# A replanned transformer-block kernel: RMS weight as a scale of its own, splits kept off GpSimd, logits with the router weights stationary

## Chip, cores, metric

One core of a Trainium2 chip. The metric is the device time of one launch in microseconds (us). All input arrays of the reference are float64 or float32 on the host; the large matmuls run as three matmuls of `float32r` parts ("hi" and "lo", x = hi + lo).

## Reference

```python
def _attn_ref(q, k, v):                       # 4 x 8 heads x 576 x 64, causal window of 64
    scores = np.matmul(q, k.transpose(0, 1, 3, 2)) / np.sqrt(D)
    scores = np.where((rel >= 0) & (rel < 64), scores, -1e9)
    attn = softmax(scores)
    return np.matmul(attn, v)
def _moe_ref(x, w_gate, w_val, w_out, rms_g): # 2304 tokens, 512 -> 1536 -> 512
    xn = x / np.sqrt(np.mean(x * x, -1, keepdims=True) + 1e-6) * rms_g
    g = xn @ w_gate
    return (g / (1 + np.exp(-g)) * (xn @ w_val)) @ w_out
def _moe2_ref(x, w_gate, w_output_gate, w1, w2):  # 8 experts, 512 -> 1024 -> 512
    logits = x @ w_gate
    e_idx = np.argmax(logits, axis=1)             # one expert per token
    ...
    out[mask] = gate_w[mask, None] * eom[mask, e, None] * (np.maximum(x[mask] @ w1[e], 0) @ w2[e])
```

## The kernel before

The 2304 tokens are 18 tiles of 128. Three parts follow each other and overlap at the seams.

**Attention** (`attention_front`, `attention_tile`), tile by tile: q, k and v are loaded (`rx`) and split into hi and lo; scores of half the heads go to a PSUM bank; max, exp with row sums, the division; four transposes; the product with V; an evacuation into `x`. Early tiles (t < `qzt`) use full 128-row weights for the scores (lines 672 to 674, and for t < `mpe` the mask is added by a 13th matmul, line 661); later tiles use two 64-row halves of TensorE (line 700, twelve matmuls for half the heads). The norm then squares (`sqr`), sums with a matmul against ones (line 850; from t >= `spe` on after two additions), takes the root by a seed and two Newton steps on 128x1 columns (`newton`, line 883 and on), transposes the result over the partitions (line 900), multiplies (`norm`, line 906) and splits into `xn`.

**Feed-forward** (`ffn_group`, `ffn_step`): seven units of 2 or 3 tiles in six groups; group 0 holds units 0 and 1. A step takes one of 12 slices of the 1536 columns: twelve matmuls for the gate, twelve for the value (lines 1050 to 1052: "a group of twelve" below; there are 168), tanh on ScalarE, two multiplications on VectorE, a split into `h`, and matmuls with `wo` (lines 1092 to 1094) into banks that stay open. In group 0 every slice's weights arrive as float64 words and are rebuilt by `conv` with integer operations on ScalarE and VectorE, split, and saved to DRAM (`whd`) for the later groups.

**Experts**: `route` transposes each finished tile (line 1160), evacuates it, multiplies with the 16 router columns `rw` (line 1167), and works out an expert and a slot for each token; GpSimd scatters the rows to DRAM (`xs`, line 1249). `experts` then runs a first block of 256 tokens, and one block per expert (the first of 128 tokens, `narrow`). `weights` loads an expert's matrices in halves and splits each half into `w` (lines 1477 to 1484); `put` scatters finished rows to the output from GpSimd's queue (line 1640). The router's last matmuls, the counting and the token loads of the blocks all lie between the last feed-forward step and the first expert block.

**What sets the order.** The code records operations (`pl.op`) with a priority, the engines that may run each and a cost on each. `Plan.order` lists them in time with these costs, gives each to the engine that would end it first, and writes the program in that order. Each engine runs its own list in order, so an instruction that waits holds all behind it. Up to a planned time `warm` the planner fills TensorE's idle time with matmuls of ones (line 505, "fillers"). `K` holds the numbers that steer it. The helpers `hi_i` (line 348 on ScalarE, 350 on GpSimd, 352 on VectorE), `lo_i` and `both` (355) and `times` (358) record all splits and many other operations, so those lines stand for many tiles' work.

Of the kernel before, what the change touches and what calls it, by code (L numbers as in the profile page):

```python
# [21 lines left out]
P = 128  # L22
# [10 lines left out]
HOP = 0.2  # L33
TICK, FULL = 3.4133, 1.275
HOPS = {"t": 0.0, "a": 0.12, "v": 0.12, "p": 0.12, "s": 0.0}
K = dict(
    qzt=6, spe=4, lact=12, warm=50, wf=1.17, flead=37.337, pvt=5, nwv=0, port=1, t0=44.466, pp=93.644,
    lead=1.877, clead=14.32, stag=6.769, stage=1.089, slack=0.045, mpe=5, nt=2, look=-0.002, marg=0.239, dw=2.625, ewl=20.108,
    ews=5.63, xld=30.179, xtn=3.067, mlead=8, vb=0.61, vb2=0.298, tb=124.917, share=-0.071, rlead=4.252, span=0.82, wl=3.695,
# [17 lines left out]
class Op:  # L57
    __slots__ = ("engs", "fn", "prio", "seq", "succ", "need", "deps", "bufs", "eng", "start", "end", "dma", "done", "dur", "rows", "lock")


class Filler:


    def __init__(self, fn, lo):
        self.fn, self.lo = fn, lo


class Plan:
# [10 lines left out]
    def op(self, engs, fn, r=(), w=(), hold=(), prio=0.0, dma=0.0, after=(), rows=1.0, lock="p"):  # L79
        o = Op()  # L80
        o.engs, o.fn, o.prio, o.seq, o.dma, o.rows = engs, fn, prio, len(self.ops), dma, rows
        o.lock = lock
# [33 lines left out]
    def order(self):  # L116
# [11 lines left out]
        def enable(o):  # L128
            for e in o.engs:
                t = max((d.end + (HOPS[e] if d.eng == e and not d.dma else HOP) for d in o.deps), default=0.0)  # L130
                heapq.heappush(wait, (t, o.seq, e, o))
# [6 lines left out]
        ticks = {}  # L138

# [29 lines left out]
        while left:  # L169
# [5 lines left out]
            for e in free:  # L175
# [3 lines left out]
                while ready[e]:  # L179
                    it = heapq.heappop(ready[e])  # L180
# [33 lines left out]
                    if e == "t":  # L214
                        c = pe_time(now, c, o.rows)
# [13 lines left out]
                    for b in o.bufs:  # L229
                        b.left -= 1  # L230
                        b.end = max(b.end, o.end)
                        if not b.left:
                            b.slot["buf"], b.slot["free"] = None, b.end + HOP
# [10 lines left out]
            if self.filler and free["t"] <= now + 1e-9 and self.filler.lo < now < K["warm"]:  # L244
# [26 lines left out]
def attention_ffn_moe(  # L271
# [102 lines left out]
    def cost(n, kind):  # L374
        f = n / 512.0
        return {
            "hs": {"a": 0.12 + 0.48 * f, "p": 0.1 + 0.52 * f, "v": 0.09 + 0.29 * f},
            "ls": {"v": 0.09 + 0.555 * f, "p": 0.17 + 1.12 * f},
            "hp": {"a": 0.1 + 0.48 * f, "v": 0.08 + 0.56 * f},
            "lp": {"v": 0.08 + 0.56 * f},  # L380
# [16 lines left out]
    rw = fixed("rw", [P, KD, 2 * E])  # L397
    iota_m = fixed("iota_m", [P, PT, E])
# [3 lines left out]
    def c_ident(e):  # L402
        t = ident.t
        nc.gpsimd.memset(t, 0.0)
# [4 lines left out]
    def c_masks(e):  # L409


        nc.gpsimd.memset(masks.t, 0.0)
# [12 lines left out]

    def c_ones(e):
# [1388 lines left out]
```

## Time and profile before

| | |
|---|---|
| median of 3 runs | 885.95 us (883.63 to 887.12) |
| profiled execution, its own time | 887.55 us |
| its span, first to last instruction | 885.5 us |
| busy: TensorE (PE) / VectorE (DVE) / ScalarE (ACT) / GpSimd (POOL) | 855.3 / 548.3 / 400.5 / 298.9 us |
| mean granted TensorE clock | 0.981 |
| instructions | 16016 |

A matmul's row shows when it starts and how long it is under way; matmuls overlap, so what one costs is the distance from its start to the next start.

### The profile page before, as it was taken

To read this page: it belongs to the slowest core of one execution; us is meant where nothing else is said; L and a number is where in the kernel's file an instruction comes from. 1 tells how busy PE (TensorE), PEld (TensorE's weight loads), DVE (VectorE), ACT (ScalarE), POOL (GpSimd) and SP (SyncE) were. 2 spreads that over 40 slices of the span, in tenths; PEclk is the share of its full clock that TensorE was granted. 3 is DMA by queue.
4 is the path that set the end of the run, shared out by engine and by line. 5 is a ranking of instruction groups with operands and counts; after the bars stand their busy time and mean duration, and the time that the engine had idled before them with its cause. 6 is when DMAs were issued, how large, how long until landed. Compare 5 with 4: busy or idle time off the path is not lost. (4 is left out here: it accounts for less than half of the span.)

```text
span 885.5 us, 16016 instructions
## 1 busy us (share of the span) xinstructions
PE 855.3 (97%) x5786; PEld 780.3 (88%) x5786; DVE 548.3 (62%) x1258; ACT 400.5 (45%) x1050; POOL 298.9 (34%) x510
## 2 busy tenths in 40 slices
PE   8989999999999999999999999999989999999995
PEld 8978998999899999889998999999968888989984
DVE  6887898977775673756466553554576253556640
ACT  7888776664643452445342342222333132343420
POOL 6886543315324231443224220210133132233320
PEclk8998999999999999999999999999998999999998
DMA  6266799637524431265014317540095344656500
GB/s 195 92 246 219 245 277 316 236 120 253 188 80 140 174 131 38 96 201 172 8 67 160 143 49 285 171 175 1 27 321 206 119 144 147 210 176 228 192 25 19
DMA packets 54016, 139.28 MB, mean 157 GB/s; under 512 B 6800, under 2 KB 6800, under 8 KB 53936
## 3 DMA queue, kind: packets, MB, share of 16 engines
q1 hardware_dynamic: 50912, 128.40, 42.9%
q0 software_dynamic: 3024, 9.85, 2.9%
q8 instruction: 46, 0.75, 0.4%
q14 instruction: 34, 0.28, 0.1%
HBM read 113.69 MB, written 24.54 MB: 156 GB/s over the span
## 5 line engine op out<-in xcount | busy, mean ns | idle before, releaser
L1050 PE MATMUL bank<-xn,w 128*128 128x384 f32 (+1 forms) x672 | 216.6, 322 | 3.3 <-POOL xn L350 2.3
L1051 PE MATMUL bank<-xn,w 128*128 128x384 f32 (+1 forms) x672 | 211.4, 315 | 0.6 <-DVE xn L355 0.6
L1052 PE MATMUL bank<-xn,w 128*128 128x384 f32 (+1 forms) x672 | 211.6, 315 | 0.2 <-DVE w L355 0.2
L1050 PEld LDWEIGHTS bank<-xn,w 128*128 128x128 f32 x672 | 128.1, 191 | 8.2 <-POOL xn L350 2.5
L1051 PEld LDWEIGHTS bank<-xn,w 128*128 128x128 f32 x672 | 128.2, 191 | 2.9 <-DVE xn L355 0.8
L1052 PEld LDWEIGHTS bank<-xn,w 128*128 128x128 f32 x672 | 128.0, 190 | 0.4 <-DVE w L355 0.4
L355 DVE TENSOR_TENSOR w<-raw,w 128x512 fp32r<-128x512 f32 x114 | 85.3, 790 | 10.7 <-POOL w L350 5.7
L1092 PE MATMUL bank<-wo,h 128*128 128x512 f32 x216 | 87.4, 405 | 1.3 <-POOL h L350 1.1
L1094 PE MATMUL bank<-wo,h 128*128 128x512 f32 x216 | 85.2, 394 | 0.0
L1093 PE MATMUL bank<-wo,h 128*128 128x512 f32 x216 | 85.0, 394 | 0.0
L1075 DVE TENSOR_TENSOR u<-u,bank 128x384 f32<-128x384 f32 (+1 forms) x84 | 41.5, 494 | 69.1 <-PE bank L1052 67.1
L1062 ACT ACTIVATE u<-bank 128x384 f32<-128x384 f32 (+1 forms) x84 | 37.2, 443 | 84.2 <-PE bank L1052 74.8
L350 POOL TENSOR_SCALAR w<-raw 128x512 fp32r<-128x512 f32 x59 | 36.3, 631 | 107.0 <-PE bank L1052 39.1
L1622 PE MATMUL bank<-w,eh 128*128 128x512 f32 (+1 forms) x168 | 67.9, 404 | 3.4 <-DVE eh L355 3.4
L1588 PE MATMUL bank<-xT,w 128*128 128x256 f32 (+4 forms) x224 | 68.5, 306 | 0.3 <-DVE eh L1599 0.3
L348 ACT CAST h<-u 128x384 fp32r<-128x384 f32 (+1 forms) x68 | 31.9, 470 | 80.2 <-DVE u L1075 74.1
L1590 PE MATMUL bank<-xT,w 128*128 128x256 f32 (+4 forms) x224 | 68.2, 304 | 0.0
L1589 PE MATMUL bank<-xT,w 128*128 128x256 f32 (+4 forms) x224 | 68.1, 304 | 0.0
L1067 DVE SCALAR_TENSOR_TENSOR u<-u,bank 128x384 f32<-128x384 f32 (+1 forms) x84 | 41.4, 493 | 42.1 <-ACT u L1062 41.5
L1624 PE MATMUL bank<-w,eh 128*128 128x512 f32 (+1 forms) x168 | 67.2, 400 | 0.0
L1623 PE MATMUL bank<-w,eh 128*128 128x512 f32 (+1 forms) x168 | 67.1, 400 | 0.0
L348 ACT CAST w<-raw 128x512 fp32r<-128x512 f32 x67 | 38.9, 618 | 35.1 <-PE bank L1052 17.4
(262 smaller groups left out, 1856.3 us busy)
## 6 DMA issues: line engine op xcount, KB each, us to landing
w<-whd SPq DMA_DIRECT2D x80, 512.0 KB, 3.8
raw<-in_moe_w_dram SPq DMA_DIRECT2D x64, 512.0 KB, 4.6
whd<-w SPq DMA_DIRECT2D x24, 512.0 KB, 5.1
raw<-in_moe_w_gate_dram SPq DMA_DIRECT2D x12, 512.0 KB, 5.4
raw<-in_moe_w_val_dram SPq DMA_DIRECT2D x12, 512.0 KB, 4.3
raw<-in_moe_w_out_dram SPq DMA_DIRECT2D x12, 512.0 KB
rx<-in_q_dram SPq DMA_DIRECT2D x18, 256.0 KB, 3.1
rx<-in_k_dram SPq DMA_DIRECT2D x18, 256.0 KB, 2.8
```

The source lines that it names most:

```text
L348: nc.scalar.copy(o, i)
L355: ve[e].tensor_tensor(out=o, in0=i, in1=h, op=ALU.subtract)
L1050: nc.tensor.matmul(o, lhsT=h_, rhs=xn.t[:, 0, kk], start=(kk == 0), stop=False)
L1051: nc.tensor.matmul(o, lhsT=h_, rhs=xn.t[:, 1, kk], start=False, stop=False)
L1052: nc.tensor.matmul(o, lhsT=l_, rhs=xn.t[:, 0, kk], start=False, stop=(kk == KD - 1))
L1092: nc.tensor.matmul(o, lhsT=h.t[:, 0, c], rhs=wo.t[:, 0, f], start=(n == 0), stop=False)
L1093: nc.tensor.matmul(o, lhsT=h.t[:, 0, c], rhs=wo.t[:, 1, f], start=False, stop=False)
L1094: nc.tensor.matmul(o, lhsT=h.t[:, 1, c], rhs=wo.t[:, 0, f], start=False, stop=(n == NF - 1))
L1588: nc.tensor.matmul(o, lhsT=wh, rhs=x.t[:, 0, kk, 0:N], start=(kk == 0), stop=False)
L1589: nc.tensor.matmul(o, lhsT=wh, rhs=x.t[:, 1, kk, 0:N], start=False, stop=False)
L1590: nc.tensor.matmul(o, lhsT=wl, rhs=x.t[:, 0, kk, 0:N], start=False, stop=(kk == KD - 1))
L1622: nc.tensor.matmul(bk.t[0:M], lhsT=hh, rhs=wh, start=(f == 0), stop=False)
```

## The change

The planner gets other costs (`LAT`, the wait after an operation by the engine that ran it; costs of splits, exp, evacuations), a price `SW` for changing between 64-row and 128-row matmuls, and a rule that keeps 64-row matmuls together (`stk`). GpSimd's cost for splits is raised by 9 us (`phs`, `pls`), so that they are no longer given to it. All of `K` is new. The norm weight `g_sb` is multiplied into `x` by an operation of its own (`weigh`) that needs only `x`, and `norm` becomes one VectorE multiplication instead of four. For the first four slices of the feed-forward weights (`sf`), the low word is moved by two halfword operations on ScalarE (`c5`, `c6`) instead of one, and VectorE's two combining operations become one shift and one combination (`c7`, `c8`). The logits are computed with the split router weights `rws` as the stationary operand (32 columns) and the token tile, split as well, as the moving one; the 32x128 result is evacuated, transposed back and its two halves added (`r2l`, `r3` to `r6`). Tile 6 uses the early form of the scores, tiles 5 and 6 the mask by matmul, and tile 4 the sum of squares by four matmuls.

```diff
 K = dict(
-    qzt=6, spe=4, lact=12, warm=50, wf=1.17, flead=37.337, pvt=5, nwv=0, port=1, t0=44.466, pp=93.644,
-    lead=1.877, clead=14.32, stag=6.769, stage=1.089, slack=0.045, mpe=5, nt=2, look=-0.002, marg=0.239, dw=2.625, ewl=20.108,
+    qzt=7, spe=5, lact=12, warm=60, wf=1.17, flead=25.12, pvt=5, nwv=3, port=1, t0=51.748, pp=92.284,
+    lead=1.956, clead=25.385, stag=6.317, stage=0.717, slack=0.051, mpe=7, nt=2, look=-0.026, marg=0.132, dw=0.933, ewl=14.362,
...
-            "hs": {"a": 0.12 + 0.48 * f, "p": 0.1 + 0.52 * f, "v": 0.09 + 0.29 * f},
-            "ls": {"v": 0.09 + 0.555 * f, "p": 0.17 + 1.12 * f},
+            "hs": {"a": 0.07 + 0.49 * f, "p": 0.09 + 0.53 * f + K["phs"], "v": 0.09 + 0.29 * f},
+            "ls": {"v": 0.08 + 0.56 * f, "p": 0.15 + 1.13 * f + K["pls"]},
...
+                        c = pe_time(now, c + SW * (o.tiled != tiled), o.rows)
...
+        def weigh(e):
+            if e == "a":
+                for kk in range(KD):
+                    nc.scalar.activation(out=x.t[:, kk], in_=x.t[:, kk], func=AF.Copy, scale=g_sb.t[:, kk:kk + 1])
+            else:
+                both(e, x.t, x.t, g_sb.t.unsqueeze(2).to_broadcast([P, KD, P]), ALU.mult)
...
         def norm(e):
-            for kk in range(KD):
-                nc.vector.scalar_tensor_tensor(
-                    out=x.t[:, kk], in0=x.t[:, kk], scalar=g_sb.t[:, kk:kk + 1], in1=bk2.t[:, 0:P],
-                    op0=ALU.mult, op1=ALU.mult,
-                )
+            both("v", x.t, x.t, bk2.t[:, 0:P].unsqueeze(1).to_broadcast([P, KD, P]), ALU.mult)
...
+        def c6(e):
+            nc.scalar.copy(t.t.bitcast(U16)[:, 1::2], a.t.bitcast(U16)[:, 3::4])
...
-            def r3(e, bx=bx, b2=b2):
+            def r3(e, bx=bx, bl=bl, b2=b2):
                 for kk in range(KD):
-                    nc.tensor.matmul(
-                        b2.t[:, 0:2 * E], lhsT=bx.t[:, kk * P:(kk + 1) * P], rhs=rw.t[:, kk],
-                        start=(kk == 0), stop=(kk == KD - 1),
-                    )
+                    for z, b in enumerate((bx, bl)):
+                        nc.tensor.matmul(
+                            b2.t[0:4 * E, 0:P], lhsT=rws.t[:, kk].rearrange("p z e -> p (z e)"),
+                            rhs=part(b)[:, kk * P:(kk + 1) * P], start=(kk + z == 0), stop=(kk + z == KD),
+                        )
```

How instructions move, at three places.

GpSimd's list, from the last scatter of routed rows to the fifth `put` (`out_dram<-osb`), before; `w<-raw` are splits of expert weights:

```order
L1249 DMA xs<-raw_7913,si_115 18432x514
L350 TENSOR_SCALAR w_8206<-raw_8143 128x512
L350 TENSOR_SCALAR w_8233<-raw_8150 128x512
L1640 DMA out_dram<-osb_8222,meta_0_148 2304x512
L1640 DMA out_dram<-osb_8281,meta_1_149 2304x512
L350 TENSOR_SCALAR w_8335<-raw_8230 128x512 x2
L355 TENSOR_TENSOR w_8337<-raw_8239,w_8337 128x512
L350 TENSOR_SCALAR w_8401<-raw_8271 128x512 x2
L350 TENSOR_SCALAR w_8422<-raw_8304 128x512
```

and the same place in the changed program:

```order
L1308 DMA xs<-raw_8099,si_118 18432x514
L1699 DMA out_dram<-osb_8425,meta_0_151 2304x512
L1699 DMA out_dram<-osb_8439,meta_1_152 2304x512
L1699 DMA out_dram<-osb_8626,meta_0_153 2304x512
L1699 DMA out_dram<-osb_8872,meta_0_154 2304x512
```

The splits of expert weights have left GpSimd's list; in this stage it holds only puts. They stand in the lists of ScalarE and VectorE.

ScalarE's list, the rebuilding of the first slice of gate weights (`t2k`, `t`), in the early attention, before:

```order
L348 COPY val_191<-val_275 64x1024
L948 ACTIVATE t2k_342<-raw_242 128x512
L953 ACTIVATE t_344<-raw_242 128x512
L730 ACTIVATE s_290,m_350<-bank_289,m_350 128x128 x4
L348 CAST kt_304<-rx_286 128x4x2x64
```

and now:

```order
L358 COPY kt_422<-kt_301 128x8x64
L969 ACTIVATE t2k_441<-raw_368 128x512
L985 ACTIVATE t_443<-raw_368 128x512
L988 COPY t_443<-raw_368 128x512
L745 ACTIVATE s_425,m_476<-bank_424,m_476 128x128 x4
```

One more ScalarE operation per rebuilt block, for 12 blocks.

TensorE's list, the logits of the first two routed tiles (`rw` the router weights, `t2k` the turned tile), before:

```order
L819 MATMUL bank_3044<-p_2984,val_1187 64x128 x2
L819 MATMUL bank_3044<-p_2984,val_1378 64x128 x2
L1167 MATMUL bank_3054<-rw,t2k_2992 128x16 x4
L1167 MATMUL bank_3064<-rw,t2k_3001 128x16 x4
L1160 MATMUL bank_3074<-ident,raw_2977 128x128 x4
```

and the head of one tile's logits now (`t2k` its hi, `t` its lo part; six more such rows follow), behind a feed-forward group:

```order
L1092 MATMUL bank_3096<-xn,w_2362 128x256
L1093 MATMUL bank_3096<-xn,w_2362 128x256
L1094 MATMUL bank_3096<-xn,w_2362 128x256
L1216 MATMUL bank_3123<-t2k_3074,rws 32x128
L1216 MATMUL bank_3123<-t_3075,rws 32x128
```

Each tile has eight matmuls of 128 columns in place of four of 16, and a transpose further down.

## Rows read from the trace of the kernel before

**Rows 1.** The page: busy time of each engine over the span.

```profile
PE 855.3 (97%) x5786; PEld 780.3 (88%) x5786; DVE 548.3 (62%) x1258; ACT 400.5 (45%) x1050; POOL 298.9 (34%) x510
```

**Rows 2.** Windows: stretch, length, busy us of engines, granted clock, DMA share, GB/s.

```profile
0.00:88.00 88.00, 77.98 (x757) 74.64 (x758) 68.35 (x132) 72.83 (x212) 65.41 (x122) 0.88 0.56 188
55.60:71.30 15.70, 11.88 (x81) 10.75 (x81) 13.63 (x30) 14.67 (x46) 9.86 (x20) 0.85 0.64 223
188.00:636.00 448.00, 443.71 (x2987) 411.65 (x2986) 261.36 (x677) 177.88 (x513) 119.80 (x245) 1.00 0.37 128
664.80:670.80 6.00, 6.00 (x17) 4.73 (x17) 3.27 (x8) 0.62 (x1) 0.62 (x1) 0.50 0.87 316
```

**Rows 3.** Waits of TensorE, 0 to 90 us: for whom; us, times, longest.

```profile
PE bank L900 <- POOL y L358: 2.5, 2, 1.5
PE bank L1050 <- POOL xn L350: 2.3, 1, 2.3
PE bank L661 <- POOL masks L423: 2.1, 1, 2.1
```

**Rows 4.** Waits of TensorE, 90 to 636 us.

```profile
PE bank L1092 <- POOL h L350: 1.1, 2, 0.6
PE bank L900 <- POOL y L358: 1.0, 2, 0.8
```

**Rows 5.** TensorE's timeline around the logits, and around 300 us: start, us, what.

```profile
196.12 0.64 PE L1160 MATMUL bank<-ident,raw 128*128 128x128 f32 x4
196.52 0.36 PE L1050 MATMUL bank<-xn,w 128*128 128x256 f32 x1
...
198.03 0.96 PE L1167 MATMUL bank<-rw,t2k 128*128 128x16 f32 x8
198.84 0.36 PE L850 MATMUL bank<-ones,xf 128*128 128x2 f32 x2
...
300.25 1.12 PE L819 MATMUL bank<-p,val 128*64 128x128 f32 x16
301.21 0.39 PE L1050 MATMUL bank<-xn,w 128*128 128x384 f32 x1
```

**Rows 6.** TensorE's timeline: early scores with their mask, later scores.

```profile
17.52 0.38 PE L661 MATMUL bank<-masks,ident_b 128*128 128x512 bf16 x1
...
19.21 0.62 PE L763 MATMUL bank<-ident,s 128*128 128x128 f32 x4
...
152.62 0.28 PE L1052 MATMUL bank<-xn,w 128*128 128x256 f32 x1
152.83 0.91 PE L700 MATMUL bank<-kt,q_all 64*128 64x192 f32 x12
153.68 0.50 PE L1092 MATMUL bank<-wo,h 128*128 128x512 f32 x1
```

**Rows 7.** Groups by form, whole span: busy us, mean ns | idle before, releasers.

```profile
L355 DVE TENSOR_TENSOR w<-raw,w 128x512 fp32r<-128x512 f32 x114 | 85.3, 790 | 10.7 <-POOL w L350 5.7 <-ACT w L348 4.3
L355 DVE TENSOR_TENSOR p<-bank,p 128x512 fp32r<-128x512 f32 x36 | 24.3, 685 | 6.9 <-ACT p L348 6.8
L352 DVE CAST w<-raw 128x512 fp32r<-128x512 f32 x2 | 0.9, 427 | 0.0
L953 ACT ACTIVATE t<-raw 128x512 int32<-128x512 uint16 x36 | 23.9, 667 | 1.2 <-DVE w L355 1.1
```

**Rows 8.** Between feed-forward and experts: puts' landing (min/median/max); timelines of POOL, DVE, PE.

```profile
DMA to landing us min/median/max: 2.7/5.0/8.5
657.93 0.97 POOL L1640 DMA_INDIRECT out_dram<-osb,meta  x1 [8.02 <-ACT osb L1553]
658.93 1.22 POOL L350 TENSOR_SCALAR w<-raw 128x512 fp32r<-128x512 f32 x2
659.60 4.53 DVE L355 TENSOR_TENSOR w<-raw,w 128x512 fp32r<-128x512 f32 x3 [4.11 <-POOL w L350]
664.78 0.80 PE L1622 MATMUL bank<-w,eh 128*128 128x512 f32 x1 [3.40 <-DVE eh L355]
```

More of the change, by code (lines that the diff above doesn't have):

```diff
@@ L57, with __init__ @@
 class Op:
-    __slots__ = ("engs", "fn", "prio", "seq", "succ", "need", "deps", "bufs", "eng", "start", "end", "dma", "done", "dur", "rows", "lock")
+    __slots__ = ("engs", "fn", "prio", "seq", "succ", "need", "deps", "bufs", "eng", "start", "end", "dma", "done", "dur", "rows", "lock", "tiled")
 class Filler:
-    def __init__(self, fn, lo):
-        self.fn, self.lo = fn, lo
+    def __init__(self, fn, lo, after):
+        self.fn, self.lo, self.after = fn, lo, after
 class Plan:
@@ L129, in enable @@
             for e in o.engs:
-                t = max((d.end + (HOPS[e] if d.eng == e and not d.dma else HOP) for d in o.deps), default=0.0)
+                t = max((d.end + (0.0 if d.eng == e == "t" else LAT["s" if d.dma else d.eng]) for d in o.deps), default=0.0)
                 heapq.heappush(wait, (t, o.seq, e, o))
@@ L178, in order @@
                 skip = []
-                while ready[e]:
-                    it = heapq.heappop(ready[e])
+                first = None
+                if e == "t" and tiled and K["stk"]:
+                    first = min((x for x in ready[e] if x[2].tiled and not x[2].done), default=None)
+                    if first is not None and first[0] < min(x[0] for x in ready[e]) + K["stk"]:
+                        ready[e].remove(first)
+                        heapq.heapify(ready[e])
+                    else:
+                        first = None
+                while ready[e] or first is not None:
+                    it, first = (heapq.heappop(ready[e]), None) if first is None else (first, None)
                     o = it[2]
@@ L243, in order @@
                 continue
-            if self.filler and free["t"] <= now + 1e-9 and self.filler.lo < now < K["warm"]:
+            if self.filler and self.filler.after.done and free["t"] <= now + 1e-9 and self.filler.lo < now < K["warm"]:
                 if ticks.get(int(now / TICK + 1e-9), 0.0) < FULL * K["wf"]:
@@ L397, in attention_ffn_moe @@
     rw = fixed("rw", [P, KD, 2 * E])
+    rws = fixed("rws", [P, KD, 2, 2 * E], F32R)
+    lgt = [fixed(f"lgt{i}", [P, P]) for i in range(2)]
     iota_m = fixed("iota_m", [P, PT, E])
@@ new lines, in r5, with r6 @@
+            def r5(e, lt=lt, b3=b3):
+                nc.tensor.transpose(b3.t[:, 0:P], lt.t, ident.t)
+            def r6(e, lt=lt, b3=b3, j=j):
+                hi_i(e, tt_["lg"][:, j], b3.t[:, 0:2 * E])
+                both("v", tt_["lg"][:, j], b3.t[:, 2 * E:4 * E], tt_["lg"][:, j], ALU.add)
+            pl.op({"t": 0.43}, r1, r=[(a, 0), ident], w=[bk], hold=[bx, bl], prio=pr, rows=0.5)
+            pl.op({"a": 0.52, "v": 0.63}, r2, r=[bk], w=[bx], prio=pr)
+            pl.op({"v": 0.63}, r2l, r=[bk, bx], w=[bl], prio=pr)
@@ L1643, in put @@
                 )
-            pl.op({"a": 0.6, "v": 0.64}, scaled, r=[bk, m], w=[o], prio=pr)
-            puts.append(pl.op({"p": 0.75}, put, r=[o, m], dma=0.73, prio=pr, after=puts[-1:]))
+            pl.op({"a": 0.55, "v": 0.61}, scaled, r=[bk, m], w=[o], prio=pr)
+            puts.append(pl.op({"p": 1.0}, put, r=[o, m], dma=0.73, prio=pr, after=puts[-1:]))
         return pr
```

177 lines of the change are left out of this document (104 added, 73 removed).

## Prediction

> **What bounds the kernel now.** I read the page's busy times first: TensorE is busy for 97% of the span, no other engine for more than 62% [rows 1]. So the sum over TensorE's own instructions decides, and an operation taken from another engine is worth only what TensorE waits for it. Next I read by stage, in windows. In the long middle, 188 to 636 us, TensorE is busy 443.7 of 448.0 us at full clock: only 4.3 us are idle there [rows 2]. The losses lie at two places. The first is the start: until 88.0 us, where the tenth of the 168 groups of twelve begins, the mean granted clock is 0.88, ScalarE is busy for 72.8 us, VectorE for 68.4 and GpSimd for 65.4 [rows 2]; much of what keeps TensorE busy there is fillers (182 matmuls before, 234 now, counted in the order). The second is the seam between feed-forward and experts, where TensorE idles 3.4 us at one instruction and then runs 6.0 us at a granted clock of 0.50 [rows 2, 8].
>
> Whom TensorE waits for is in its wait view. Up to 90 us the three longest waits all end with GpSimd: 2.5 us for the root of the norm, 2.3 for a split of `xn`, 2.1 for the masks [rows 3]. Between 90 and 636 us GpSimd ends 1.1 and 1.0 us [rows 4]. At the seam, GpSimd's list holds splits of expert weights behind a put. The put stood idle for 8.02 us [rows 8]; the instruction named as its releaser belongs to the next block, and puts take up to 8.5 us to land, so I read it as waiting for the put before it. The splits start only then; VectorE, which takes their low parts, idles 4.11 us, needs 4.53 us for three of them, and TensorE gets `eh` 3.4 us late [rows 8].
>
> **The change, part by part.**
>
> *Logits.* Eight rows of one tile's logits run from 198.03 to 198.84: 0.81 us. The new form has eight matmuls of 128 moving columns with few stationary ones; the nearest row is line 819, sixteen in 0.96 us, so 0.060 each and 0.48 for a tile. A transpose is 0.10 (four in 0.40) [rows 5]. Per tile 0.81 - 0.48 - 0.10 = 0.23, times 18: 4.1 us less. The longer chain (a low part, an evacuation, an addition more) runs beside feed-forward groups; if that cover is short, TensorE waits at the transpose, by at most a VectorE operation of 0.685 us [rows 7] per routed unit, so 5 us in seven units at the outside. I take nothing: the order puts a feed-forward group between nearly all of these steps.
>
> *Attention on TensorE.* Tile 6 has two early score groups of 1.69 us (17.52 to 19.21) for two later ones of 1.06 (152.62 to 153.68) [rows 6]: 1.3 more. The mask matmul of tile 5 is what 1.69 has over twelve matmuls of 0.11 (an estimate, a little over a transpose's 0.10 [rows 5]): 0.37, twice: 0.7. Tile 4's sums are three matmuls more, each two rows in the trace and priced as a transpose row: 0.6. Together 2.6 more; the VectorE operations that they replace were not waited for.
>
> *64-row groups.* The order has 20 stretches of line 700 before and 13 now; two of the seven went with tile 6. Before such a stretch stand 0.21 us, where neighbours of the same form stand 0.12 apart (twelve from 196.52 to 198.03 give the same) [rows 5, 6]. With as much at its end, an estimate, five times 0.18 is 0.9 less.
>
> *The start.* Ahead of the tenth group, ScalarE's list grows from 172 to 207 instructions, VectorE's from 132 to 198; GpSimd's falls from 129 to 42. Thirty-five ScalarE instructions at the mean of 72.83/212 would be 12.0 us [rows 2]; the twelve halfword copies are dearer (0.667 us for their nearest kin [rows 7]), so I take 14, and 87 us of ScalarE work ahead of that point. In exchange TensorE has done about 6 us more there: 24 more score matmuls, six more with `wo`, a transposed root. So the kernel before is at the same point of TensorE's work at 94 us. In its fullest stretch ScalarE is busy 14.67 of 15.7 us, 93% [rows 2]: that gives 93.5 us. At its share over the whole start (83%) it would be 105, at 97% 90. What speaks for the upper end: masks come earlier, since GpSimd no longer clears them, and the root's 2.5 and the split's 2.3 leave GpSimd [rows 3]. I take 2 us less, with the ends 6.9 less (all of rows 3) and 11 more.
>
> *The middle.* GpSimd's 2.1 us go [rows 4]; VectorE, busy 261 of 448 us [rows 2], takes on about a quarter more by the count of its list, and stays under three quarters. I take 2 us less; ends 4.3 less (all the idle time there) and 4.3 more (as much again).
>
> *The seam.* With GpSimd's list free of splits, nothing that TensorE needs stands behind the waiting put: VectorE's pairs get their high parts from VectorE and ScalarE, also without the slowing that shows in the low parts of weights (790 ns against 685 for a form that has no GpSimd partner) [rows 7]. Removed are the 3.4 us and the half of 6.0 us lost to the low clock, 6.4 in all [rows 2, 8]. What is late next: the first expert's token tile. In the new order its transposes are followed at once by the matmuls that need their high and low parts; one ScalarE and one VectorE operation of some 0.7 us each [rows 7] then lie open, and the last scatters have two TensorE groups less to hide behind. That gives back 2 us: 4.4 less, ends 6.4 and 0.
>
> *The sum.* -4.1 + 2.6 - 0.9 - 2 - 2 - 4.4 = -10.8. The profiled execution took 887.55 us: 876.8. It lies 1.6 us above the median of the three runs, 885.95; against that the sum is 875.2, and I say **875 us**.
>
> **A rule against the change.** The new lists hold some fifty VectorE casts of weights from SBUF to SBUF, of which the trace has two (0.427 us each) [rows 7], and routed rows still leave through GpSimd. If each of the last unit's three scatters waited for one such cast, the tokens would come 1.3 us later, and the time would be 876.5.
> The Trainium skill ("SBUF — State Buffer", section "SBUF: two separate sides") says that GpSimd cannot write the descriptors of its own DMAs while VectorE runs a copy in a two-port mode, since the two share a port pair. By its figures, about 620 ns alone and 3100 ns beside such copies, the three would lose some 7 us, an estimate, and the sum would be 882; no row of this trace shows it.
>
> **The rivals.**
> - *The start goes as planned.* All of rows 3 and all of the seam are saved: -2.4 - 6.9 - 2 - 6.4 = -17.7, so 868 us. For it: fillers last longer and keep the clock up. Against it: ScalarE would have to be busy for 97%.
> - *ScalarE becomes the bound of the start.* At 88% busy the tenth group is at 99 us, 5 us late: 875 + 2 + 5 = 882, no change to speak of. For it: its list there is 14 us longer while its room is the same.
> - *Slower.* The same place at 80%, a little below the 83% of the whole start [rows 2]: 87/0.80 is 109 us, 15 late, and 875 + 2 + 15 = 892. It decides from 107 us on, a share of 81%. Against it: of what ScalarE waited for, GpSimd's part is gone.
> - *Scatters starved by casts*, as above: 876.5.
> - That the splits do not leave GpSimd can be left out: the order shows that they did.
>
> **How the numbers follow.** Chances: the forecast 0.50 (own range 870 to 880), start as planned 0.17, ScalarE bound 0.16, slower 0.10, starved scatters 0.07. The measurement can tell about 0.5% from no change, 4.4 us: 881.5 and 890.4. Forecast, planned start and starved scatters fall below 881.5, less a little for their upper ends: faster 0.71; ScalarE bound and these ends: same 0.18; slower 0.11. The range must hold 8 in 10: from 866, a little under the planned start, to 886, over the bound start; the ends of the middle (4.3) and of the seam fall inside it.
>
> **What would show it.** In the changed profile: eight logit matmuls of a tile in about 0.5 us; no wait of TensorE for GpSimd in the start and the middle; the tenth group at 90 to 96 us, ScalarE busy over 90% ahead of it; no idle 3.4 us and no half clock at the seam, but some 2 us before the first expert's matmuls; POOL busy well under 100 us. The prediction is wrong if the tenth group comes after 100 us, if the seam still loses over 5 us, or if VectorE's fuller list opens new waits in the middle of more than 5 us.

## The result, and the profile after

The changed kernel takes 873.22 us (median; 871.59 to 874.02, 4 executions), the kernel before beside it 885.16 us (883.63 to 887.12): a ratio of 0.9862, 95% interval 0.9835 to 0.9888. That is 1.4% faster, well over the 0.5% that can be told from no change. The profiled execution took 872.55 us, 15.0 less than that of before (887.55), where the sum in the prediction had 10.8 less; the medians are 11.9 apart.

Line numbers have moved: the gate and value matmuls are L1092 to L1094 now, the first expert's L1606 to L1608, the logits L1216, the helper that copies on ScalarE L358, on GpSimd L360, on VectorE L362, the one for low parts L365, for products L368. First the page's busy line (engine, busy us, share of the span, instructions), to be held against [rows 1]:

```profile
PE 848.8 (97%) x5866; PEld 778.4 (89%) x5866; DVE 610.3 (70%) x1567; ACT 446.0 (51%) x1161; POOL 79.9 (9%) x120
```

GpSimd has about a quarter of its work left (79.9 of 298.9 us); VectorE is busy for 62 us more and ScalarE for 45.5. TensorE's share has not changed: it bounded the kernel before and does now. So the gain must be found in its stages. The view of windows gives them: the stretch up to the tenth group of twelve, from there to the first expert matmul, from there to the wide products of the experts, and from there to the last matmul. First the changed kernel's:

```profile
core 0: us, PE busy (x) PEld busy (x) DVE busy (x) ACT busy (x) POOL busy (x), PEclk, DMA share, GB/s
0.00:97.30 97.30, 86.64 (x847) 82.58 (x848) 85.02 (x198) 86.98 (x250) 11.92 (x42) 0.89 0.55 182
97.30:616.10 518.80, 518.18 (x3599) 483.47 (x3598) 381.34 (x1011) 268.25 (x732) 38.87 (x52) 1.00 0.47 157
188.00:636.00 448.00, 447.70 (x3092) 417.32 (x3091) 314.91 (x905) 208.27 (x592) 37.38 (x53) 1.00 0.37 132
616.10:658.90 42.80, 40.96 (x264) 35.53 (x263) 29.27 (x113) 15.85 (x35) 5.12 (x7) 1.00 0.43 140
658.90:861.90 203.00, 203.00 (x1161) 176.83 (x1159) 114.68 (x247) 74.23 (x145) 23.06 (x18) 1.00 0.47 167
```

The same stretches of the kernel before (its first, up to 88.0 us, is in [rows 2]):

```profile
88.00:624.00 536.00, 529.98 (x3613) 490.74 (x3612) 349.06 (x831) 244.12 (x670) 159.04 (x297) 1.00 0.46 154
624.00:670.80 46.80, 41.79 (x249) 35.90 (x248) 30.30 (x108) 14.97 (x33) 11.46 (x15) 0.93 0.59 206
670.80:876.60 205.80, 205.48 (x1174) 179.00 (x1172) 100.56 (x189) 67.86 (x135) 62.02 (x75) 1.00 0.42 147
```

| stretch of TensorE | before | after | difference |
|---|---|---|---|
| up to the tenth group | 88.0 | 97.3 | +9.3 |
| to the first expert matmul | 536.0 | 518.8 | -17.2 |
| to the wide products | 46.8 | 42.8 | -4.0 |
| to the last matmul | 205.8 | 203.0 | -2.8 |

These make -14.7. The first two rows belong together: the changed kernel has done about 6 us more work at its tenth group (the prediction's estimate), so by that estimate the start is 3.3 us late, and the second stretch 11.2 us shorter. In that stretch TensorE idles 0.6 us (518.80 less 518.18), 6.0 before: 5.4 of the 11.2. It is also busy for 11.8 us less; with some 4 for the logits and the forecast 0.9 for the 64-row stretches, about 7 are left for work done earlier, so the estimate of 6 is not far off. In 188 to 636 us alone, 0.3 us are left of the 4.3 of [rows 2].

Next the wait view of TensorE, up to 98 us (line, what was waited for, us in all, times, longest), against [rows 3]:

```profile
PE warm L520 <- DVE ones_b L442: 2.8, 1, 2.8
PE bank L874 <- ACT xf L857: 2.6, 3, 1.2
PE bank L1092 <- ACT xn L358: 2.3, 1, 2.3
PE bank L778 <- DVE s L368: 1.4, 1, 1.4
```

GpSimd is gone from the list, but the waits are not: the 2.3 us for a split of `xn` stand at the same matmul as before, now behind ScalarE. The seam and the logits, from TensorE's timeline (start, us, line, tiles, idle before):

```profile
644.27 0.50 PE L1606 MATMUL bank<-w,xT 128*128 128x512 f32 x1 [1.54 <-DVE xT L365]
```

```profile
204.04 0.27 PE L1225 MATMUL bank<-ident,lgt 128*128 128x128 f32 x1
204.06 0.30 PE L1216 MATMUL bank<-t2k,rws 128*32 128x128 f32 x1
204.20 0.23 PE L1216 MATMUL bank<-t,rws 128*32 128x128 f32 x1
...
204.62 0.60 PE L1202 MATMUL bank<-ident,raw 128*128 128x128 f32 x4
```

The 3.4 us of [rows 8] and the low clock behind them are gone; 1.54 us are idle ahead of the narrow expert's first product. The eight logit matmuls run from 204.06 to 204.62, 0.56 us, and with the transpose from 204.04, 0.58, where [rows 5] have 0.81. Last, the groups by shape for VectorE and GpSimd (count, busy us, mean ns, idle before):

```profile
L365 DVE TENSOR_TENSOR w<-raw,w 128x512 fp32r<-128x512 f32 x128 | 82.7, 684 | 0.5 <-ACT w L358 0.2
L1699 POOL DMA_INDIRECT out_dram<-osb,meta x21 | 26.0, 1237 | 203.0 <-ACT osb L1692 169.6 <-DVE osb L1694 12.7 <-issue 10.5
```

### The profile page after: what moved, and what is told of

The parts are those of the page before. It is cut to its first block, busy times and chain, and to the rows that moved or that the text cites. A ratio compares the mean times of both kernels' runs of the same rounds, so it can differ in the third digit from the quotient of the medians.

```text
span 870.8 us, 16032 instructions
## 1 busy us (share of the span) xinstructions
PE 848.8 (97%) x5866; PEld 778.4 (89%) x5866; DVE 610.3 (70%) x1567; ACT 446.0 (51%) x1161; POOL 79.9 (9%) x120
## 4 chain that ended last, share of the span: by engine, by line
PE 78%; issue 8%; ACT 7%; DMA 3%; DVE 3%; POOL 0%; POOLq 0%; ACTq 0%; DVEq 0%
PE bank L1092 11%; PE bank L1094 11%; PE bank L1093 11%; PE bank L1134 6%; PE bank L1135 5%; PE bank L1136 5%; DMA out_dram<-osb,meta 3%; PE bank L1681 3%; PE bank L1683 3%; PE bank L1682 3%; PE bank L834 3%; PE bank L1647 2%; PE bank L1648 2%; PE bank L1649 2%; PE bank L715 2%
## 5 line engine op out<-in xcount | busy, mean ns | idle before, releaser
L1092 PE MATMUL bank<-xn,w 128*128 128x384 f32 (+1 forms) x672 | 216.0, 321 | 2.5 <-ACT xn L358 2.3
L1094 PE MATMUL bank<-xn,w 128*128 128x384 f32 (+1 forms) x672 | 211.0, 314 | 0.0
L1092 PEld LDWEIGHTS bank<-xn,w 128*128 128x128 f32 x672 | 127.7, 190 | 6.6 <-ACT xn L358 2.5
L1094 PEld LDWEIGHTS bank<-xn,w 128*128 128x128 f32 x672 | 127.7, 190 | 0.0
L365 DVE TENSOR_TENSOR w<-raw,w 128x512 fp32r<-128x512 f32 x128 | 82.7, 684 | 0.5 <-ACT w L358 0.2
L358 ACT CAST h<-u 128x384 fp32r<-128x384 f32 (+1 forms) x74 | 34.4, 465 | 70.7 <-DVE u L1117 70.5
L1681 PE MATMUL bank<-w,eh 128*128 128x512 f32 (+1 forms) x168 | 67.0, 399 | 0.0
L1683 PE MATMUL bank<-w,eh 128*128 128x512 f32 (+1 forms) x168 | 66.3, 394 | 0.0
L1682 PE MATMUL bank<-w,eh 128*128 128x512 f32 (+1 forms) x168 | 66.2, 394 | 0.0
L358 ACT CAST w<-raw 128x512 fp32r<-128x512 f32 x74 | 44.7, 618 | 34.1 <-PE bank L1094 14.1
L1653 ACT ACTIVATE eh<-bank 128x256 fp32r<-128x256 f32 (+4 forms) x64 | 26.7, 418 | 55.1 <-PE bank L1649 51.4
```

The lines of the kernel that those rows point to most:

```text
L1092: nc.tensor.matmul(o, lhsT=h_, rhs=xn.t[:, 0, kk], start=(kk == 0), stop=False)
L1094: nc.tensor.matmul(o, lhsT=l_, rhs=xn.t[:, 0, kk], start=False, stop=(kk == KD - 1))
L1681: nc.tensor.matmul(bk.t[0:M], lhsT=hh, rhs=wh, start=(f == 0), stop=False)
L1682: nc.tensor.matmul(bk.t[0:M], lhsT=hh, rhs=wl, start=False, stop=False)
L1683: nc.tensor.matmul(bk.t[0:M], lhsT=hl, rhs=wh, start=False, stop=(f == NF2 - 1))
```

## The experiments

**How they are compared.** Executions of one and the same program differ by 7 us (the changed kernel) or more (8.8 in e1). In the changed kernel they go with the mean granted clock of the span: it took 867.3 us at 0.995, 871.6 and 872.2 at 0.987, 872.6 to 872.7 at 0.985 and 873.9 to 874.3 at 0.981 (ten executions). So beside medians I compare executions of equal clock. This is a rough measure: the kernel before took 882.7, 884.8 and 887.6 us at 0.983, and e3 876.0 at 0.987 but 878.3 at 0.988. The versions also ran on four chips (e1 to e4, e5 to e8, e9 to e11, e12), each with the kernel before beside it, and the ratios are taken on one chip. In the table the last column compares at equal clock, against the changed kernel.

| version | median us | ratio to before, interval | mean clock of its executions | at equal clock |
|---|---|---|---|---|
| e1 expert splits on GpSimd | 873.51 | 0.9882 (0.9838-0.9927) | 0.982-0.995 | +3.3 to +6 |
| e2 other splits on GpSimd | 890.68 | 1.0067 (1.0033-1.0101) | 0.978-0.983 | +16 |
| e3 logits as before | 876.16 | 0.9902 (0.9867-0.9938) | 0.985-0.995 | +4.1 to +4.6 (+3 to +6 with two that have no partner) |
| e4 no halfwords, planned anew | 873.25 | 0.9882 (0.9844-0.9919) | 0.986-0.993 | not used |
| e5 no halfwords, same order | 874.85 | 0.9917 (0.9883-0.9950) | 0.979-0.988 | +1.4 to +3 |
| e6 more fillers | 872.72 | 0.9892 (0.9852-0.9932) | 0.980-0.995 | +0.3 to +2 |
| e7 changed kernel again | 872.67 | 0.9875 (0.9839-0.9912) | 0.981-0.995 | - |
| e8 before, splits off GpSimd | 880.60 | 0.9958 (0.9930-0.9985) | 0.978-0.987 | to before: -2 to -9 |
| e9 norm as before | 871.47 | 0.9865 (0.9830-0.9900) | 0.985-0.991 | +1.3 |
| e10 start splits on GpSimd | 870.54 | 0.9858 (0.9823-0.9894) | 0.986-0.988 | -1 |
| e11 fillers at every sum | 870.49 | 0.9861 (0.9827-0.9894) | 0.984-0.995 | +0.4 |
| e12 both | 867.82 | 0.9844 (0.9822-0.9867) | 0.993-0.998 | about 0 |

The planner turns a small edit into another order, and that alone moves the time. So most experiments leave its list as it is and alter what the entries do.

**e1, the seam: the engine or the order?** After the plan is made, the experts' splits get the engines of before.

```diff
     seq = pl.order()
+    for ops, engs in (
+        (split_hi, "apapapap..."),   # 59 on GpSimd
+        (split_lo, "vvvvvvvv..."),   # 14 on GpSimd
+    ):
+        for o, e in zip(ops, engs):
+            o.eng = e
```

> The changed kernel with its order of instructions kept; only the splits of the expert weights go back to the engines that the plan of before gave them (59 high parts and 14 low parts on GpSimd). Theory A, the seam gained because these splits left the queue in which the puts wait: TensorE waits again for a product that GpSimd's late splits hold up, 3 to 5 us at the seam or behind the first put, total about 877 (4 us over the changed kernel's 873.2), and the low parts of weights on VectorE go from 684 ns back to about 790. Rival, the seam gained by the new order (what stands ahead of what), not by the engine: TensorE waits no more than the 1.5 us of now, total 872 to 874.5.

At equal clock 871.2 to 871.8 us stand against 867.3 (0.995), 875.2 against 871.9 (0.987), and 879.3 and 879.9 at 0.984 and 0.982 lie some 6 above. The median hides this: half of e1's executions had the high clock. The windows show where it is lost; e1 first, then e7, whose start runs alike to 0.1 us up to the nineteenth group (119.0 us):

```profile
619.40:663.30 43.90, 40.99 (x263) 35.39 (x262) 27.40 (x108) 14.67 (x32) 8.86 (x12) 1.00 0.39 130
```

```profile
617.70:660.40 42.70, 40.86 (x263) 35.47 (x262) 29.20 (x113) 15.84 (x35) 5.12 (x7) 1.00 0.43 141
```

That is 1.2 us in the seam; from its end to the last matmul e1 needs 206.0 us and e7 203.1, 2.9 more. TensorE's waits there, which e7 has not, and the low parts on VectorE:

```profile
PE bank L1647 <- DVE eh L1658: 1.6, 4, 0.5
PE bank L1578 <- DMA xs<-xs: 1.1, 1, 1.1
```

```profile
L365 DVE TENSOR_TENSOR w<-raw,w 128x512 fp32r<-128x512 f32 x114 | 97.6, 892 | 28.9 <-POOL w L360 28.4
```

Low parts go from 684 ns to 892 when GpSimd makes high parts, with 28.4 us of waiting for GpSimd. So the engine matters, 4 us in this order, but the 3.4 us stall of before does not come back in one piece; that the new order puts other work ahead of it is my reading, which no run shows. Theory A holds in its total, not in its place. (Another 1.7 us between these two executions arise from 120 to 126 us, where no expert weight is split yet: a difference that the edit does not explain.)

**e2, the rest of the splits.** The same for attention and feed-forward: fourteen kinds of split get the engines of before (tile 6, whose form is new, those of its old one).

```diff
+    for kind, engs in {"k_lo": "vpvpvvpppppp...", "h_lo": "vppvpppp...", ...}.items():
+        for o, e in zip(was[kind], engs):
+            o.eng = e
```

> The changed kernel with its order kept; all splits of attention and feed-forward (not the experts') take the engines that the plan of before gave them, 118 more instructions on GpSimd. Theory A, ScalarE bounds the start (10.9 of 11.0 us busy from 55 to 99 us): with about a third of its splits gone, the tenth group of twelve comes at 93 to 95 us instead of 97.3, and the middle (188 to 636 us) idles 2 to 4 us again for GpSimd's parts of xn and h; total 871 to 876. Rival, the start is bound by the low clock between 26 and 43 us or by a chain that splits have no part in: tenth group at 97 or later, middle as in A, total 875 to 878.

Both theories fall, and far: 890.2 to 890.7 us at 0.980, where the changed kernel has 874 at 0.981. The windows up to the tenth group, from there to 188 us, and on to the last group:

```profile
0.00:107.00 107.00, 89.37 (x848) 84.77 (x849) 84.08 (x174) 84.70 (x244) 38.63 (x71) 0.89 0.50 165
107.00:188.00 81.00, 77.49 (x569) 71.48 (x568) 74.56 (x136) 60.04 (x141) 32.26 (x31) 1.00 0.77 237
188.00:626.30 438.30, 436.83 (x3003) 406.83 (x3002) 291.69 (x809) 193.11 (x561) 90.43 (x111) 1.00 0.42 142
```

The tenth group comes at 107.0, not earlier, although ScalarE is free for 22 us there (79% busy) and GpSimd does 38.6 us of the work. GpSimd is no quicker at it: in e2 a high part of `xn` takes 0.76 us there and 0.62 on ScalarE, a low part 1.29 and 0.71 on VectorE, and TensorE waits 2.7 us for one of GpSimd's parts of `xn`. Behind 188 us only 1.5 us are idle. An order is made for its engines; this one, with the engines of before, is worse than before's own, so e2 measures the misfit too and not the price of GpSimd alone.

**e3, the logits.** Only r2 to r6 of the routed tile change (r5, r6 and the low part do nothing):

```diff
-                    for z, b in enumerate((bx, bl)):
-                        nc.tensor.matmul(b2.t[0:4 * E, 0:P], lhsT=rws.t[:, kk]..., rhs=part(b)[:, kk * P:(kk + 1) * P], ...)
+                    nc.tensor.matmul(b2.t[:, 0:2 * E], lhsT=bx.t[:, kk * P:(kk + 1) * P], rhs=rw.t[:, kk], ...)
```

> The changed kernel with its order kept; the router logits are computed as before (eight matmul rows of a tile with the tokens stationary, no low part, no transpose of the logits). Theory A, the logits lie open on TensorE: the rows of a tile cost 0.84 us again in place of 0.50 and 0.06, total 5 us more than the changed kernel, about 878. Rival, they lie in time in which TensorE would have waited for the chain behind them anyway: 0 to 2 us more, 873 to 875.

871.9 against 867.3 us at 0.995, 876.0 and 876.2 against 871.6 and 872.2 at 0.987, 877.2 against 872.6 at 0.985: 4.1 to 4.6 us. Two more executions have no partner of their clock: 874.0 at 0.989 and 878.3 at 0.988 lie some 3 and 6 us above what the neighbouring clocks give. That is Theory A, about its 5; the logits lay open on TensorE.

**e4 and e5, what bounds the start: ScalarE?** In e4 the halfword conversions went back to their old form by new entries; these read other tiles, so the plan came out anew (188 fillers for 234), against what its expectation says. It says nothing on the start, and e5 does it in the old list:

```diff
         def c5(e):
-            nc.scalar.activation(out=t.t.bitcast(U16)[:, 0::2], in_=a.t.bitcast(U16)[:, 1::4], ...)
+            c0(e)
         def c6(e):
-            nc.scalar.copy(t.t.bitcast(U16)[:, 1::2], a.t.bitcast(U16)[:, 3::4])
+            c3("v")
         def c7(e):
...
+            pass
         def c8(e):
...
+            c02(e)
```

> The changed kernel with its order kept, fillers included; the twelve halfword conversions go back to the form of before: 12 copies of 0.76 us fewer on ScalarE and 12 of 0.79 that become 0.66 (10.7 us less), on VectorE two operations of 0.68 in place of 0.35 and 0.68 (4 us more). Theory A, ScalarE bounds the start: the tenth group comes 3 to 5 us earlier (92 to 94), total 868.5 to 870.5. Rival 1, VectorE is as much the bound (97% busy from 66 to 88 us): tenth group at 97 to 99, total 873 to 875. Rival 2, the chain of softmax and norm bounds it: tenth group within 1 us, total within 1 us.

> The changed kernel with its order of instructions kept in full, fillers included; the twelve halfword conversions go back to the form of before (ScalarE loses 12 copies of 0.76 us and 0.13 of each of 12 others, 10.7 us in all; VectorE has an operation of 0.68 for one of 0.35, 4 us more). Theory A, ScalarE bounds the start: the tenth group of twelve at 92 to 95 us, total 868 to 871 at the same granted clock. Rival 1, VectorE is as much the bound: tenth group at 97 to 100, total 872 to 876. Rival 2, what bounds the start is the chain of softmax and norm at the low clock from 26 to 43 us: both within 1 us of the changed kernel.

e5 is no faster with 10.7 us less on ScalarE: 873.3 us against 871.6 and 872.2 at 0.987, 875.8 at 0.984 against 872.6 at 0.985, and its tenth group comes at 98.0 us. (Of the two VectorE operations one now stands where the copy stood in the list, so VectorE's order is not quite the same.) Its windows of 44 to 88 us:

```profile
44.00:66.00 22.00, 20.03 (x243) 19.13 (x240) 21.01 (x46) 20.24 (x57) 0.00 (x0) 1.00 0.59 186
66.00:88.00 22.00, 17.68 (x145) 16.32 (x144) 21.56 (x46) 18.75 (x53) 1.04 (x1) 0.92 0.67 218
```

ScalarE has become free for 3 us of 22 and VectorE is busy for 21.56: ScalarE alone does not bound this start, and Theory A falls. Rival 1 fits the total; the tenth group, 0.7 us later, fits Rival 2 as well. This execution too was at 0.50 from 26 to 40 us, and VectorE had 4 us more to do, so e5 does not tell what ScalarE's list costs at full clock. In the changed kernel both are full from 44 to 88 us, as its windows show:

```profile
22.00:44.00 22.00, 20.81 (x175) 20.39 (x173) 15.81 (x41) 16.78 (x51) 1.04 (x1) 0.61 0.28 80
44.00:66.00 22.00, 20.40 (x256) 19.64 (x254) 20.28 (x44) 21.43 (x59) 0.00 (x0) 1.00 0.53 178
66.00:88.00 22.00, 19.15 (x158) 17.73 (x157) 21.40 (x52) 21.94 (x60) 1.04 (x1) 0.92 0.65 231
```

But from 22 to 44 us neither is: 15.81 and 16.78 of 22.0, at a granted clock of 0.61.

**e6, e11: the low clock of the start.** TensorE's timeline of the changed kernel ahead of that stretch:

```profile
21.79 0.67 PE L520 MATMUL warm<-ones_b 128*128 128x128 bf16 x9
23.65 1.05 PE L874 MATMUL bank<-ones,xf 128*128 128x2 f32 x8 [1.19 <-ACT xf L857]
```

Fillers, 1.19 us of nothing, then eight matmuls of two columns that take 1.05 us; then the granted clock falls to 0.50, which is 1.2 of 2.4 GHz, at about 26 us, and stays there until about 43 us:

```profile
27.00:43.00 16.00, 16.00 (x123) 15.79 (x122) 11.40 (x33) 11.83 (x38) 1.04 (x1) 0.50 0.18 54
```

For these 16 us TensorE itself is the full engine, and VectorE and ScalarE have room. The experiments add fillers in such places.

```diff
     seq = pl.order()
+    at, n = {9: 6, 12: 3, 13: 3, 16: 3, 17: 2}, 0      # e11: {9: 8, 12: 3, 13: 3, 16: 2, 17: 4, 27: 2, 32: 8}
+    for o in list(seq):
+        if o.eng == "t" and o.seq >= 0:                # the n-th entry of TensorE that is no filler
+            for _ in range(at.get(n, 0)):
+                x = Op()
+                x.eng, x.seq, x.bufs, x.fn = "t", -1, [], fill
+                seq.insert(seq.index(o), x)
+            n += 1
```

> The changed kernel with 34 more filler matmuls on TensorE, ahead of the first sums of squares (where it idled 1.2 us) and behind four steps of attention between 26 and 33 us. Theory B, the low clock from 26 to 43 us costs the start: with the gaps filled the granted clock stays at 1.0 there (0.61 now), the first groups of twelve come 3 to 6 us earlier, total 867 to 870. Rival, ScalarE bounds what follows anyway: the clock is kept but the tenth group stays within 2 us of 97.3, total 871.5 to 874. Second rival, fillers do not keep the clock: the added 2.6 us of matmuls show in full, total 875.

> The changed kernel with 60 more filler matmuls on TensorE, ahead of each of the first sums of squares (where it idled 1.2, 0.4 and 1.1 us, and after which the granted clock fell to 0.50 in all profiles so far but one) and behind attention steps between 26 and 33 us. Theory B, the low clock that follows these gaps is what separates executions at 867 from those at 874: with the gaps filled most executions have a mean clock of 0.99 and more and take 867 to 869. Rival, fillers cost what they save, or the clock falls elsewhere: median 872 to 875.

In e6's profiled execution the clock held:

```profile
22.00:44.00 22.00, 20.75 (x273) 20.08 (x272) 19.97 (x49) 21.52 (x69) 1.94 (x2) 1.00 0.39 111
44.00:66.00 22.00, 18.21 (x225) 17.31 (x224) 20.73 (x52) 21.85 (x58) 0.00 (x0) 1.00 0.57 199
66.00:88.00 22.00, 20.86 (x171) 19.39 (x172) 21.17 (x46) 21.88 (x64) 2.09 (x2) 0.92 0.71 229
```

ScalarE is busy for 21.52 us of 22 to 44 instead of 16.78, the tenth group comes at 92.7 us and the execution takes 868.07. Its window up to the tenth group:

```profile
0.00:92.74 92.74, 82.15 (x882) 77.87 (x882) 84.44 (x198) 86.65 (x251) 12.10 (x42) 0.98 0.59 191
```

So in this order the low clock costs the start some 5 us. It does not clear ScalarE: with the clock held that engine is busy for 93% of the start, and no run lightens its list at full clock. And only two of e6's six executions went so; two had 0.980. With fillers at all the sums (e11) four of six lie at 0.991 to 0.992 and one at 0.995: the clock that Theory B asked for, but not its time, with a median of 870.49. Its tenth group comes at 95.3 us. At equal clock these fillers cost 0.3 to 2 us; what they bring is the clock. One profile a run does not show where the clock fell in the other executions.

**e7, the changed kernel again.** No edit.

> The changed kernel once more, unaltered, beside the others on this chip: about 873 us, and repeated executions that differ by where the granted clock falls in the start, so that the time goes with the mean clock (872.5 at 0.985, 874 at 0.981 so far).

As expected, 872.67 us, and with one execution at 867.3. Its profile has the low clock three times, from 28 to 38, 62 to 75 and 92 to 96 us; the first two lie in these windows:

```profile
22.00:44.00 22.00, 20.79 (x216) 20.34 (x214) 18.16 (x45) 19.59 (x61) 1.51 (x2) 0.77 0.31 81
44.00:66.00 22.00, 20.58 (x231) 19.73 (x230) 20.71 (x51) 21.83 (x58) 0.00 (x0) 0.90 0.58 201
66.00:88.00 22.00, 20.09 (x150) 18.77 (x150) 19.30 (x43) 19.92 (x56) 1.04 (x1) 0.79 0.63 205
```

Same instructions, other stretches of low clock than in the profile above, and its tenth group comes at 98.9 us.

**e8, one part alone.** The kernel before, GpSimd priced out of splits:

```diff
-            "hs": {"a": 0.12 + 0.48 * f, "p": 0.1 + 0.52 * f, "v": 0.09 + 0.29 * f},
-            "ls": {"v": 0.09 + 0.555 * f, "p": 0.17 + 1.12 * f},
+            "hs": {"a": 0.12 + 0.48 * f, "p": 9.0 + 0.52 * f, "v": 0.09 + 0.29 * f},
+            "ls": {"v": 0.09 + 0.555 * f, "p": 9.0 + 1.12 * f},
```

> The kernel before, of which only one thing is changed: splits may no longer go to GpSimd, and the order follows from that by before's own constants. Theory A, GpSimd's splits are what the seam and the middle waited for: about 8 us less there, the start loses some of it to fuller lists of ScalarE and VectorE, total 878 to 882. Rival, without constants found for it the order does not bear the fuller lists: 886 to 895.

Theory A in its total: 880.60 us, ratio 0.9958 (0.9930 to 0.9985), which is 1 to 6 us less. Equal clock tells no more here: 879.4 and 880.5 at 0.986 against 882.0 are 2 us less, 881.7 to 882.4 at 0.978 against 891.1 are 9. The middle, the seam and the experts:

```profile
188.00:636.00 448.00, 445.18 (x3010) 414.01 (x3009) 284.87 (x748) 184.76 (x531) 61.55 (x173) 1.00 0.37 129
624.00:665.10 41.10, 38.90 (x249) 33.77 (x247) 29.04 (x112) 15.16 (x34) 6.55 (x7) 1.00 0.59 208
665.10:870.00 204.90, 204.90 (x1175) 179.02 (x1172) 112.58 (x245) 71.04 (x142) 18.54 (x18) 1.00 0.46 153
```

Its first expert matmul starts at 624.0 as in before, and the seam takes 41.1 us instead of 46.8, clock 1.00: 5.7 us from this part alone, and low parts at 682 ns. The later experts take 204.9 us (205.8), only 0.9 less, and in the middle 2.8 us stay idle, 1.5 less than before. Of before's 4.3, 1.7 were no wait for GpSimd:

```profile
PE bank L1233 <- DVE x L831: 1.7, 2, 1.4
```

**e9, the norm.** In the changed order, the operation that weighs does nothing and the four of before are in the place of the one product:

```diff
-            both("v", x.t, x.t, bk2.t[:, 0:P].unsqueeze(1).to_broadcast([P, KD, P]), ALU.mult)
+            for kk in range(KD):
+                nc.vector.scalar_tensor_tensor(out=x.t[:, kk], in0=x.t[:, kk], scalar=g_sb.t[:, kk:kk + 1], in1=bk2.t[:, 0:P], ...)
```

> The changed kernel with its order kept; the norm weight is applied as before, in four VectorE operations together with the root, and the operations that weigh are gone (ScalarE: 60 of 0.39 us fewer; VectorE: four of 0.34 for one of 0.68 in each of 18 tiles, 12 us more, 4 of it in the start). Theory, ScalarE and VectorE are both full in the start, so one operation more on the chain of each tile costs there and nothing in the middle: tenth group 1 to 3 us later, total 874 to 877 at a mean clock of 0.985 (the changed kernel: 872.6). Rival, VectorE has the room: total within 1 us of the changed kernel at the same clock. Second rival, ScalarE's relief counts for more: 870 to 871.5.

873.94 against 872.6 us at 0.985: 1.3 more, between the first theory and its rival; the tenth group is at 97.4 (97.3). Its median is 1.2 us below the changed kernel's, because three of its four executions had a clock of 0.989 or more. What the norm's new form is worth is hardly over what can be told.

**e10, e12: a version that beats both.** GpSimd may take splits again, for the first six tiles' queries and keys and the feed-forward weights only, and the plan is made anew:

```diff
-    def cost(n, kind):
+    def cost(n, kind, late=9.0):
...
-            "hs": {..., "p": 0.09 + 0.53 * f + K["phs"], ...},
+            "hs": {..., "p": 0.09 + 0.53 * f + late, ...},
...
-        pl.op(cost(512, "hs"), lambda e: hi_i(e, part(0), x(0)), ...)
+        pl.op(cost(512, "hs", 0.2), lambda e: hi_i(e, part(0), x(0)), ...)
```

> The changed kernel, planned again with one thing altered: splits of the queries and keys of the first six tiles and of the feed-forward weights may go to GpSimd again, which takes 27 more instructions, nearly all in the start. Theory, ScalarE and VectorE together bound the start while GpSimd is busy for 12 of 99 us: the tenth group comes 3 to 7 us earlier at the same clock, total about 3 us less at the same clock, 869 to 870 at 0.985. Rival, TensorE waits for GpSimd's slower splits again, as in the kernel before: total 874 to 880, waits for POOL of 2 us and more in the start.

870.54 us. The tenth group comes at 88.0 us, but this is another order with other work ahead of it; at equal clock the gain is about 1 us (871.5 at 0.986, between the changed kernel's 872.6 and 871.9). The rival's waits for GpSimd stay at 0.3 us. e12 adds 44 fillers in the gaps of e10's profile, as e11 did:

> The version with 27 splits of the start back on GpSimd, with 44 filler matmuls more in the gaps that its own profile shows in the start (0.3, 0.8, 0.3, 0.4 and 1.1 us, the last of which stood ahead of the low clock from 58 to 74 us). If both effects add: 866 to 867 in executions without a low clock, median 867 to 869, ratio to before 0.980 to 0.984. Rival, the clock falls elsewhere or the fillers delay the chain: median 870 to 872, as with either alone.

867.82 us (865.51 to 869.07), ratio 0.9844 (0.9822 to 0.9867): the fastest here, 4.9 us under e7's median; the intervals of the two ratios (e7: 0.9839 to 0.9912) overlap, and they ran on different chips. All six executions have a mean clock of 0.993 to 0.998, and the start's windows have 1.00 throughout:

```profile
22.00:44.00 22.00, 21.30 (x273) 20.30 (x270) 20.87 (x49) 20.58 (x71) 8.86 (x10) 1.00 0.39 117
44.00:66.00 22.00, 19.36 (x213) 17.72 (x213) 20.68 (x48) 21.88 (x63) 7.20 (x8) 1.00 0.64 200
66.00:88.00 22.00, 20.85 (x186) 19.62 (x184) 20.34 (x50) 21.93 (x52) 2.54 (x3) 1.00 0.74 233
```

At that clock the changed kernel takes 867.3 us too. So what is shown is that the clock is held in all six executions, where one of e7's six had it; the median is 4.9 us lower than e7's and 2.7 lower than e10's. That the splits in the start add to it is not shown.

## Why the prediction was right

The total was right (875 forecast, 873.22 measured), and in part by luck. By stage, with the estimate of 6 us, the start came out 5.3 us worse than its term (+3.3 for -2). The stretch behind it came out 6.8 better (-11.2 for -4.4, the sum of logits, attention, 64-row stretches and middle; 3.4 of that is idle time, the rest no run isolates), and the later experts 2.8 better, for which the sum had nothing. The logits and the seam came out as reasoned.

- **Logits, -4.1: right.** e3 gives 4.1 to 4.6. The rows with the transpose are 0.58 us a tile, as estimated (0.48 and 0.10), and no wait for the longer chain shows on TensorE.
- **Attention on TensorE, +2.6, and 64-row stretches, -0.9:** no run isolates them. They stay as worked out.
- **The seam, -4.4: right in size.** 46.8 us became 42.8, the clock there is 1.00, and 1.5 us (2 forecast) are idle ahead of the narrow expert's products. e8 shows that taking splits off GpSimd does it by itself (5.7 us). Whether the splits' place behind the put did the harm, as I argued, or the slower low parts on VectorE, no run separates: e1 puts the splits back and loses 1.2 us there, without the stall. What I had not seen is that the later experts gain too: 2.8 us between the two profiles and 2.9 in e1, though only 0.9 in e8.
- **The price of a low part** beside GpSimd, 790 ns against 685 by analogy: right, 684 without, 892 with the splits put back in e1. The Trainium skill ("SBUF — State Buffer", section "SBUF: two separate sides") has a port pair that GpSimd and VectorE share, locked for a whole instruction, also by a VectorE operation with two inputs from SBUF beside a GpSimd operation that reads there; the low part is such an operation, and these rows agree in direction.
- **The middle, -2: too small.** 4.0 of the 4.3 idle us went, near the end of the range that I gave it. Taking splits off GpSimd alone (e8) took 1.5 of it, near the 2 that I had for that; the rest went with the new order and costs, and no run isolates it. VectorE, at 70% there (314.91 of 448), opened no new waits: the longest there is 0.3 us.
- **The start, -2: the step that failed.** Set against the 94 us of before at equal work, it gave 3.3 us back where I took 2 off: the tenth group is at 97.3 (98.9 in e7), outside the 90 to 96 that I had named, near the rival of a bound ScalarE (99), while the total stayed where the forecast was. I let ScalarE's share decide, 87 us at 93%. The work was right (86.98 us); the share was 89%. What the share hid is the granted clock: at 0.50 from about 26 to 43 us TensorE itself is full, and ScalarE is busy for 11.83 of 16 us. In e6, with the clock held there, ScalarE has its 93% and the tenth group comes at 92.7, where I had put it. [rows 2] showed 0.88 for before; I read it and gave it no price. With 0.89 the changed kernel's start is no worse in the clock than before's; why the same clock costs the new start more than the old, no run shows.
- **The planned start (868) as a rival** described the fast end: the changed kernel's execution at 0.995 took 867.3. ScalarE at 97% over the whole start was not needed for such a time: e6's execution of 868.07 us has 93%, with the clock held.
- **Scatters starved by casts:** no. The last unit's three scatters take 0.98 to 0.99 us each. The puts take 1.24 us instead of 1.03 on the mean and 2.43 instead of 1.27 at most, and TensorE waits for none. The same section of the Trainium skill has about 3100 ns for a DMA from GpSimd's queue beside a VectorE copy; with 54 casts of weights the trace shows no put of that length, and no time lost. The five puts that take 1.76 us and more start within a run of VectorE's low parts, with no cast beside them; the longest:

```profile
703.31 2.43 POOL L1699 DMA_INDIRECT out_dram<-osb,meta  x1 [6.10 <-ACT osb L1692]
703.04 1.89 DVE L365 TENSOR_TENSOR w<-raw,w 128x512 fp32r<-128x512 f32 x3
```

## What to carry to other kernels

An operation taken off a helper engine is worth what the bounding engine waited for it, not its own length: here taking the expert splits off the queue that also holds the puts was worth 4.1 us (e1) to 6.6 us (e8) at the seam and in the experts, while the 219 us of work that left GpSimd said nothing. Before you name the busiest helper engine as the bound of a stage, take work off it in an unchanged order; if nothing moves, look at the granted clock of that stage. Compare executions at equal mean clock as well as medians, or a median tells more of the clock than of the edit; and see first how far executions of one kernel at one clock lie apart (here up to 5 us).

## What was not expected of the hardware

The granted clock is not the same in two executions of one program: the changed kernel's span had means from 0.981 to 0.995, and times from 874.3 to 867.3 us with it. In all six profiles of this order without more fillers there (changed kernel, e1, e3, e5, e7, e9) it fell from 2.4 to 1.2 GHz at 26 to 28 us, after a gap of 1.2 to 1.4 us on TensorE that eight matmuls of two columns followed, and stayed there for 10 to 17 us. But the gap does not settle it: the next gap of this kind, 1.06 us, was followed by no fall in the first profile (it ends at 63.1, and the next fall comes at 70.7, behind a wait of 2.3 us for `xn`) and by one from 62 to 75 us in e7's, where it ends at 60.5; and with the first gap filled to 0.3 us (e11) the clock still fell, from 27 to 31 us. With 34 to 60 filler matmuls more it fell less often; only in e12 had every execution a mean of 0.993 or more.

GpSimd's operations can be held up by what runs beside them: nine of its twelve products for the softmax take 1.04 us in the changed kernel, as all eleven do before, and three take 1.32 to 2.53. Each of the three starts while a VectorE operation with two inputs runs; the longest, at 98.73 us, starts within three such operations in a row.
